# Block-sparse attention and a gated convolution FFN on one core: the diagonal matrices of the last convolution made on GpSimd instead of VectorE

## The chip, the core and the metric

One core of one Trainium2 chip. Its engines work side by side and meet at semaphores: TensorE (PE, matrix products into PSUM; PEld is its loading of weights), VectorE (DVE), ScalarE (ACT), GpSimd (POOL) and SyncE (SP), which here only issues transfers. Each engine takes its instructions strictly in the order in which the program gives them. The metric is device time of one execution in microseconds. A profile is one execution, recorded by the hardware; its span runs from the first to the last instruction.

## The reference

Inputs are q, k and v of 4 batches, 8 heads, 768 positions and 64 values per head, a table of 3 sampled key blocks for each of 24 query blocks, and the weights of a feed-forward part. Attention is computed under a mask of 32x32 blocks; what follows is a ReLU, a convolution of three taps along the positions, and a gate:

```python
scores = scale * np.matmul(q, k.transpose(0, 1, 3, 2))
mask = np.abs(blk_i - blk_j) <= window
mask = mask | (blk_i == 0) | (blk_j == 0) | (blk_i == n_blocks - 1) | (blk_j == n_blocks - 1)
for qb in range(n_blocks):
    for kb in sampled_blocks[qb]:
        mask[qb * block:(qb + 1) * block, kb * block:(kb + 1) * block] = True
scores = np.where(mask, scores, -1000000000.0)
...
out = np.matmul(attn, v)          # attn: softmax of scores
...
h = np.maximum(x @ w_in, 0.0)     # x: the heads side by side, 512 wide; h: 1024 wide
for k in range(K):                # K = 3
    conv_out += conv_w[k][None, None, :] * hp[:, k:k + S, :]
gate = 1.0 / (1.0 + np.exp(-conv_out))
return (h * gate @ w_out).astype(np.float32)
```

## The kernel before

The work is written as a graph of 1,811 small steps (`op`), each with a name, the engine or engines that may run it, and the buffers that it takes and uses. Nothing is scheduled when the kernel is built: the text `ORDER` lists all the steps in the order in which they are put down, two characters for the step, one for its engine where there is a choice, and one for each buffer that it takes (`put_down`, L94). A planner with its own table of costs has searched that order beforehand; the costs and due times that stand in the `op` calls are the planner's and do nothing at run time. So an engine's queue is the list of its steps in the order of the text.

Attention goes in units: for two heads at a time (a pair P, 16 pairs in all) and half of the positions, TensorE computes scores of 128x1024 into `st` (L773; the contraction of 88 rows is the 64 values of a head and 24 rows that carry the mask), ScalarE takes their exponential into `pt` (L785, 144 of them), and TensorE multiplies them with `vt` into `av` (L810). VectorE divides by the sum (L719, L721) into `xtok`. A segment is half a batch; the last half of the last batch is cut into one segment of 256 and one of 128 positions. For each segment `xtok` is transposed, multiplied with `winb` into `mix` (L914), put through the ReLU into `hE` (ScalarE L934 or VectorE L936), convolved and gated into `gT` (VectorE L972, L980, L1022, L1027, ScalarE L1019), multiplied with `woutb` (L844), copied to `o2s` and stored.

Keys and queries come in through GpSimd's transfer queue into `nat`. For the first pairs TensorE transposes them into `mix` or `av` and VectorE copies them into the slot `t` (L328 is the helper line for all plain copies of VectorE, L324 that of ScalarE, L326 that of GpSimd); later pairs are transposed by transfers into `stg` and copied from there. v comes into `vn` and is copied into `vt`. GpSimd's queue holds the issues of these loads (L239) in a fixed sequence; between them stand copies of one element, `pace` (L419, L685), that read a buffer and so keep a load from starting before that buffer has been written. In the first 15 us TensorE's queue also has 42 dummy products on `warm` (L230), of which the last 29 are named `fill`.

The convolution is done on VectorE, three multiplications with a tap each and two additions. In the last segment of 128 positions alone TensorE does it: for each of the 8 blocks of 128 channels and each of the 3 taps it multiplies `hE` with a diagonal matrix `diag` of 128x128, which carries the tap's weights of the channels (L991, 24 products). These 24 matrices are made by the steps `diag`, eight of them with three instructions each (L391): the identity `ident` times a column of `cw`. `cw`, the weights turned by one small transpose through `mix` (L381, L383), is ready at about 11 us, and the order puts the eight steps at 11.8, 13.1, 21.9 (two), 23.8, 26.9 (two) and 58.2 us.

Of the kernel before, what the change touches and what calls it, by code (L numbers as in the profile page):

```python
# [22 lines left out]
5l05m0z0T1ZV11+V5n21/020V21V5q15r5v01m11VV01n0W1t0ZV1u5s35w0A5e05f0B5E15F5x45G55j5k5o5J05K2a05L02bV22d12eV2fV2cV5O1
5P5p5t0C0D5Q15T05U0E1R15u0F0G0H5y6016127V15A014V5B1SV1TV5V25z16235H2n2k22y02g22A14V2B4W1w2u34X2M14Y2O04Z2P1x4+6505I
662o05M6742pV32qV6a16b6c55N5R2r16f06g5S5W5X2302sV2tV6k16l2lV2175Y15Z5C15DV024V630642zV325V1q6h06m16t06u68696d6e6y1
6z6i6j6v26A36n6o16D06E2h16F45+06w6I16J6x6B6C6G6R06S6H6K56L6M6W16X6T06Y11v1a2iV6p21r6q2jV6N05/V6O6r16/0706U06V6sV6P0
6QV71274175763in1io7907aiq0ir7i17j7b41p1sipV001d2NV4isViL07k51y4/2+2it17n07oiu6Z6+7p0iMiNiOivV1501z513025231531A54
1B5537056iP7s17t7273iw0ix7x07y2v17u1iyA393103211e330347z277787G17H7c2C02wV2xViT12DV47e12EViU7f7L07M7d17l7I37N4iQiF1
7Q17m7RiG7q7r7V07W7v7wiHV22F07AiR2GV2HV7S57X07B2Q17+17/7J0iz080187088892iA7K8c18d8e32RV0iWiViS0iBV32SV7C27O7P7T8h0
8i7U7Y7Z2T0iX2UV7D8m18j48n818302VViC18v0iDiEV8wiI0821iJiYiZ84iKVi/2j0j738o58x08A18B8a8b8f8g8F08G8C18H28k7g18l8p8q  # L30
8K17E08L8y08P08z7hA18M38518Q8D8E8I8R48r1j2i+7FVj18s86V8X18J8Y8Z58N8O8t0900912/V0j8j38Sja8uV8U235Vj9jl1951jm8T192096
8+8/939a09b94jf0jgj497136Vjbj538V1j69c2jc9i1989j9n0999o9d9ejhjn9k43c19p58Vjd9f0je9s19t9u1573a583b23d113g13hV2593i
3j12I03l3k5a3r3u3v02W13n08W2joji9x09yjjA0jpV19g3eV3fV1o9z39C1jr1jsju0jvjtAjwAjP09l09m9D2J19q9K09Ljx09E0jy9P19Q9M2
9R49r9v9wjQ2KV2LVjzVjSjR9A9U09V9B9FjA19H1jT9W59IjBjCAjX19Z19G19N9+jD0jG1jHa50jEjU9/1jZjVjYjFVj+a6jIAa739Oaa19Sabac0
jM12X09Taf0ag9XjN9Yak1alah4k322YVk42ZVk6j/am5jJ0ap0jKa0aqa1a80a9adax1aeaiajay3x3s23w3G3Dk0k5jLVa22jOVjWk1kb3a3k7k2
kckdkear2anaz1aoaC0aDaskp0aH1aIat1aAaE3aJ0k8aBaM0aFaNaGkB1aU1aKkCaLkqaVaO4aZ0aPaQa+kfkgaW5a/2k9kakrkDb219h9J3o3z13A
3m3a43y4au0khkiksb3kEktA2b433pV3BVkFV3avb70kK0b8kLb90kH13CV3qVbc1aX0kIbdaYkJV14kMAbe53H23E03J3I3S3P3Q13T33Vbk0blkQ0
b0kN1bm1b1kRb5kSAl30aR1l4aSl6l5l7kOkPA5lb1ld3tV3b6bp1bqbr4bakT0bu0bbl83L1jkkukG3M3W0aw03K0aT3UbvkW1kUkVV6bz1bw2bAbf
bg1kXbnbokYAbB3bsbH0kZ0bIbtbxk+bM1bybNl01bJ0k/A7lclj2lklml9bR0bCbSl1kj0bO5bh2lebil2V3FV43NVla1lflr3bW1bXbT1bY4kv1bD
kkb/0bK03RA0bE0llbFlslnc0c71c8c13kwbLbPbQbUkxbVbZb+c90lgcc0cdklkyce53XkzA0bGbjkAjqlulhltlvkmc2c31cach1cbciknV2lo3+  # L40
414213/24643lic41lplwlx3OVlqcj2lF1lz0cm0cnlGlAcu1cvcw1co4lBlHly3YV1lIlJV3cz1lClDV0cAcfcB3cE0lO1cFlPlL03ZVc540V1lQV
cG0lMlNAcgcJ1cKm70cO0cPckcllU1cpcqlVm8m9macr0cL5lR0lSmbcscQ2lWAlTAmf1mccx0cW1cycXcCc/0cDl+1l/d0cHcIcMcNcY4d41d5d13
d65mhmgmdmim0VcRcT2mjlX0lYcS1lZAcZd90c+m11dadh1d2dim40d3m2d7mkdb2dj3dm0dnm5d8dr1ds44454c4f4g04k4h4imemn2momlmqcUm3V
m6VmpkolKc61471lE4l048cVctdo1mJ1dcdw0dxdddk0dldt0dy4mv3mxmrmmmwde1mydfmzdB1dCdpmD0dqdJ0dKdumKdD5msdL3mEdO1dvdzdAdE
dF1dPmtmu4d04t4u2mAdT0dUdMmFdNmLdgdQ1dV0dRdY1mBmCmMdZmGe40dSe5mNV1dG2d+4dWdXm/1e91n04eV249V24aVn1V084j4y4q4r1e65
mHA2eaee0d/e0eb2n50efn21n34mmO4sV3dHe10e24z1dI2eg3ej1ekn6e70eo0epn4Vnn0n7V9np4nV3no4oVel1eq04v4H4I34w4x4E4M4J4F24K
4Lne1e8ew1ecexn80n9ey5edeheieB0nfeCemenereG1eHnaAeD2ngAnb0es1ezeL0nceMeAnh1nv1nqet1eI34S4T0eN1eunrndVanwnD2nxnEny
eT1eEeUnk0eFnieJeKeOePeY0nleV4eZnjAbnseQ2eRnGnz4pe3ev4AeS4N04Oe+0eW0f11nmAf2mP1eXmQe/mRf60f0f7mV0f35f4mSnAf82fb1mW
nFnL3nMnHnBntnOnNmTV3nP4GV44BV4nu0nCnIfcfd1fj0mXfkf5mYfl4fo1f9oc1fpft0odmZA0nQfq0oeVnJo90fafufeoao31obAfg0nK4CVo4
o5Afy1fzo60o7nZ1n+oz0nRfv3fA5o8AoAnSfhoBor1otosoC4PV0ouoDov4QVfG0fHff1n/o0fI2fL1fMoi0fmfnfQ0fRo1A1ojfrof1ogfsfN1fw  # L50
fxfV1fWfS4okAohAoEoH2owfX0nT0ol1fBfCfJ0f+0f/g03fKomfOfPnUg61fTg7g85nVoIoxonVoJoyoFoKgb0gcoo1opfUfD1oLfYfZgg1ghg1nW
oqVfE4UV0gd2o2fi0m+4b4DfFmU4RoMgi1oP3oQg32oGoRoSg4oTgl0gmg21gn4p11g9gt1gugagep2gfgjgy0gkgzgogv0nXA1gA3oUgpgw0gxoX0
gD1gEgM0gBoYgF5gq0groNoOoVoWgNgCp3oZgR1gSgO2gGgHgP1o+gT1o/A0p4gW0gXgY4h31h4gI1gJp5V3gK0pd1pepfpgh80gLV1gsg5nYh9gQ
h50phA1p0mIp6ha3pj0pm1pkpnplA1cpoApH1pIpJpKhd1hehf5hm0pp0ps1pqptgUhnhr1gVprAdpuAgZpy0g+h60h7ho2pLpMpP0g/0pQpRpNpSh0
hbhspv1hw0pzhcht1hxpwhghhpAApxAepThi2pX2pYhjp+pO1pZhy4hF1pB0pChGp71p8pDAfp9hK0h10pahp1hLhqhuhvhH0pUpVp/h2ApbA0hzhA
hk0hB1hlVpE1pFhM3hChT1hD0hUi00hI0hJpGApWhEVq33q0q4q5q6q1qq1hNhP0hO1i1qw0qrhV5i22qsAgq7q8hWq2i51i6hXhY2ie0ifqH1q9qb1
qxqcqdqaig1qyAhhZqIqX0hQqKqYqeqn0qoi31i4i74i8qfA2qpAii90hR1ihiihSA2ia1ibqz2qAqBqCij0qDikqt0ic1quidAqh1qvAjqih+0qj
h/Ail0qkqEimAqlA3rl0rmrnAqP3qQqFqJqGqLq+qSqRrr1rsrtAqMrx1ru0rvryro1rprH0rwArz2qNqTrAqOqZrBrIr30rqArC1rDr4r91raqgpc
piqmqUrE1rJ2q/qVr0rFqWrGr1rKrM1sd0s71rNrbr5s8serO3r2rLrPrcrQrdA2s9r6r7V0rR1rSsfrTrUsasgrf0rgrVA1sbA3shArer8rWscsirh
rirjArkrX1rYrZr+s11r/Vs0s2s3s4s5As6  # L60
"""


# [49 lines left out]
def kernel(  # L113
# [149 lines left out]
    o_ident = op("ident", {"POOL": 0.31}, lambda e: nc.gpsimd.affine_select(  # L263
        out=ident, in_=ident, compare_op=ALU.not_equal, fill=1.0, base=0,
        pattern=[[-1, 128]], channel_multiplier=1), -19, [o_imem], after=[o_iota])
# [120 lines left out]

    o_diag = {}
    for f in sorted({f for prs in CONV_PE.values() for pr in prs for f in (2 * pr, 2 * pr + 1)}):
        def dg(e, f=f):
            for x in range(3):  # L390
                nc.vector.tensor_scalar(out=diag[:, x, f], in0=ident, scalar1=cw[:, x, f:f + 1], scalar2=None,  # L391
                                        op0=ALU.mult)
# [683 lines left out]
```

## Time and profile before

| | |
|---|---|
| median of 3 runs | 207.18 us (206.76 to 207.27) |
| the profiled execution | 207.02 us |
| its span | 205.2 us |
| granted TensorE clock, mean | 0.998 |
| busy, TensorE | 200.1 us, 98% of the span |
| busy, ScalarE | 189.4 us, 92% |
| busy, VectorE | 184.7 us, 90% |
| busy, GpSimd | 60.0 us, 29%; nothing after 133.9 us |
| the 24 instructions L391 on VectorE | 4.6 us together |
| TensorE's first use of a diagonal matrix | 192.7 us |

Busy time is the union of the instructions' spans on an engine. A row of the timeline gives start, length, engine, line, operation, what is written and read, and how often; in brackets the idle time ahead of it and what ended that. A group's row gives busy time, the mean length of one in ns, and idle time ahead. A row of the chain gives start, length and what the end of the program waited for there. A busy TensorE is not one at its peak, since the ends of its instructions are modelled.

### The profile page before, as it was taken

The numbers are of one execution on the slowest core, as the hardware profiler recorded it, in microseconds if no ns is written. First come the engines' busy times: TensorE is split into PE (matmuls) and PEld (weight loads), VectorE is DVE, ScalarE is ACT, GpSimd is POOL, SyncE is SP. The second block draws the span as 40 slices with busy tenths as digits, with TensorE's granted clock in tenths as the row PEclk, the third lists the DMA queues.
The fourth block names the chain that finished last, engine by engine and source line by source line (L and its number), as shares of the span: only waits on it lengthen the run. The fifth ranks groups of instructions, "written<-read, shape, count | busy, mean of one in ns | idle before, by whom it ended". The sixth has DMA issues, their size and how long they took to land.

```text
span 205.2 us, 6315 instructions
## 1 busy us (share of the span) xinstructions
PE 200.1 (98%) x2442; PEld 145.2 (71%) x2442; DVE 184.7 (90%) x577; ACT 189.4 (92%) x252; POOL 60.0 (29%) x116
## 2 busy tenths in 40 slices
PE   7999999999999999999999999999999999999994
PEld 5678877877677766766477667766676767787773
DVE  6999999999999998999899979999999737999970
ACT  5899999999999999999799999999999989998843
POOL 5987634326242423114215334710000000000000
PEclk9999999999999999999999999999999999999999
DMA  6999997999989995999969779994040260001305
GB/s 148 191 179 193 188 201 119 143 120 148 144 110 113 124 143 73 244 123 127 222 106 171 116 103 180 133 136 77 0 139 21 78 227 0 3 0 71 139 29 179
DMA packets 50913, 25.45 MB, mean 124 GB/s; under 512 B 35588, under 2 KB 48740, under 8 KB 50884
## 3 DMA queue, kind: packets, MB, share of 16 engines
q0 software_dynamic: 20000, 11.24, 44.5%
q1 hardware_dynamic: 30452, 13.45, 32.8%
q8 instruction: 19, 0.31, 0.6%
q10 hardware_dynamic: 432, 0.36, 0.6%
q14 instruction: 10, 0.08, 0.1%
HBM read 23.09 MB, written 6.29 MB: 143 GB/s over the span
## 4 chain that ended last, share of the span: by engine, by line
PE 78%; ACT 14%; DVE 4%; issue 3%; ACTq 0%
PE st L773 25%; PE mix L914 18%; PE mix L844 15%; PE av L810 13%; ACT pt L785 10%; PE av L230 2%; DVE t L328 2%; ACT hE L934 2%; ACT m L1019 1%; PE st L844 1%; PE mix L740 1%; PE av L991 1%; ACT o2s L324 1%; DVE diag L391 1%; PE mix L536 1%
## 5 line engine op out<-in xcount | busy, mean ns | idle before, releaser
L785 ACT ACTIVATE pt<-st 128x1024 bf16<-128x1024 f32 x144 | 140.3, 1033 | 4.5 <-PE st L773 3.3
L773 PE MATMUL st<-t 88*128 88x256 bf16 (+2 forms) x600 | 93.0, 268 | 0.5 <-ACT pt L785 0.3
L810 PEld LDWEIGHTS <-pt 128*128 128x128 bf16 x1152 | 55.4, 97 | 13.7 <-ACT pt L785 0.4
L773 PEld LDWEIGHTS <-t 88*128 88x128 bf16 x600 | 48.6, 97 | 20.6 <-issue 1.0
L810 PE MATMUL av<-vt,pt 128*128 128x65 bf16 x1152 | 62.4, 193 | 0.1
L914 PE MATMUL mix<-xT,winb 128*128 128x384 bf16 (+2 forms) x288 | 55.7, 308 | 0.1
L972 DVE TENSOR_SCALAR m<-hE,cw 128x382 bf16<-128x382 bf16 (+2 forms) x192 | 49.9, 318 | 3.8 <-ACT hE L934 3.6
L844 PE MATMUL mix<-woutb,gT 128*128 128x512 bf16 (+2 forms) x200 | 49.6, 360 | 0.0
L980 DVE TENSOR_TENSOR m<-m 128x764 bf16<-128x764 bf16 (+2 forms) x64 | 33.4, 531 | 0.2
L914 PEld LDWEIGHTS <-winb 128*128 128x128 bf16 x288 | 24.1, 97 | 8.6 <-issue 0.7
L1019 ACT ACTIVATE m<-m 128x764 bf16<-128x764 bf16 (+2 forms) x32 | 26.2, 826 | 0.0
L844 PEld LDWEIGHTS <-gT 128*128 128x128 bf16 x224 | 18.7, 97 | 8.8 <-DVE gT L1027 0.3
L419 POOL COPY pace<-pt 1x1 bf16<-1x1 bf16 x24 | 7.6, 317 | 50.3 <-ACT pt L785 50.1
L934 ACT ACTIVATE hE<-mix 128x384 bf16<-128x384 f32 (+2 forms) x39 | 18.9, 504 | 0.9 <-PE mix L914 0.4
L721 DVE TENSOR_TENSOR xtok<-av,rcp 128x384 bf16<-128x384 f32 (+2 forms) x36 | 18.2, 507 | 0.3
L1027 DVE TENSOR_TENSOR gT<-m,hE 128x764 bf16<-128x764 bf16 (+3 forms) x36 | 18.0, 508 | 0.3
L239 POOL DMA_DIRECT2D nat<-in_q_dram x23 | 16.9, 736 | 2.0 <-issue 1.6
L936 DVE TENSOR_SCALAR hE<-mix 128x384 bf16<-128x384 f32 x25 | 13.8, 554 | 1.0 <-PE mix L914 0.7
L328 DVE COPY t<-mix 64x384 bf16<-64x384 bf16 (+1 forms) x34 | 13.8, 410 | 0.8 <-PE mix L536 0.2
L1022 DVE TENSOR_SCALAR m<-m 128x764 bf16<-128x764 bf16 (+3 forms) x36 | 12.1, 342 | 0.6 <-ACT m L1019 0.5
L239 POOL DMA_DIRECT2D vn<-in_v_dram x16 | 11.5, 720 | 1.3 <-issue 0.6
L328 DVE COPY t<-stg 64x1536 bf16<-64x1536 bf16 x20 | 11.6, 586 | 0.3
(74 smaller groups left out, 118.9 us busy)
## 6 DMA issues: line engine op xcount, KB each, us to landing
out_dram<-o2s SPq DMA_DIRECT2D x16, 256.0 KB
vn<-in_v_dram POOLq DMA_DIRECT2D x16, 192.0 KB, 5.1
nat<-in_k_dram POOLq DMA_DIRECT2D x15, 192.0 KB, 5.0
out_dram<-o2s SPq DMA_DIRECT2D x15, 128.0 KB
nat<-in_q_dram POOLq DMA_DIRECT2D x6, 192.0 KB, 4.9
winb<-in_moe_w_in_dram POOLq DMA_DIRECT2D x2, 512.0 KB, 7.6
woutb<-in_moe_w_out_dram POOLq DMA_DIRECT2D x4, 256.0 KB, 7.3
nat<-in_q_dram POOLq DMA_DIRECT2D x9, 96.0 KB, 4.9
```

Of the source, the lines that this page charges most:

```text
L239: return op(name, {eng: occ}, lambda e: on(e).dma_start(out=dst(), in_=src), prio, deps, dma=(kind, service), **kw)
L328: nc.vector.tensor_copy(out=dst, in_=src)
L721: nm = op("norm", {"DVE": t_dps(128 * C)}, lambda e: nc.vector.tensor_tensor(out=xtok_t[xk.index][:, 0:C].rearrange("p c h d -> p h c d"), ...
L773: nc.tensor.matmul(out=st[:, 128 * x:128 * (x + n_)], lhsT=t[0:88, 12 + 6 * hh + kc, :], rhs=t[0:88, idx:idx + (n_ - 1) * (2 if P < NPE el ...
L785: nc.scalar.activation(out=pt_t[ptb.index][:, c0:c1], in_=st_t[stb.index][:, c0:c1], func=AF.Exp, bias=0.0, scale=0.125)
L810: nc.tensor.matmul(out=o[:, off:off + 65], lhsT=pt_t[ptb.index][:, 128 * x:128 * x + 128], rhs=V_t[vslot_b[P].index][:, hh, kc, 0:65], sta ...
L844: nc.tensor.matmul(out=acc(), lhsT=gT_t[gb.index][:, ffc, 128 * t:128 * t + 128], rhs=woutb[:, ffc, c0:c1], start=(ffc == 0), stop=(ffc == ...
L914: nc.tensor.matmul(out=mix_t[hb.index][:, w1 * y:w1 * y + w1], lhsT=winb[:, fc, 128 * ffc:128 * ffc + 128], rhs=xT_t[xt_buf[n].index][:, f ...
L934: nc.scalar.activation(out=dst, in_=src, func=AF.Relu, bias=0.0, scale=0.5)
L972: nc.vector.tensor_scalar(out=m_t[cb.index][:, x, y, 0:w], in0=hE_t[heb.index][:, f0 + y, t0 + x:t0 + x + w], scalar1=cw[:, x, f0 + y:f0 + ...
L980: nc.vector.tensor_tensor(out=m[:, a_, :, 0:w], in0=m[:, a_, :, 0:w], in1=m[:, b_, :, 0:w], op=ALU.add)
L1019: th = [op("tanh", {"ACT": t_act(2 * w) + 0.04}, lambda e, cb=cb, w=w: nc.scalar.activation(out=m_t[cb.index][:, 0, :, 0:w], in_=m_t[cb.in ...
```

## The change

The step `diag` goes from VectorE to GpSimd, and its place in the order from the first third to the end of GpSimd's queue, behind the last load of v. The order of the first third was searched again with that.

```diff
-                nc.vector.tensor_scalar(out=diag[:, x, f], in0=ident, scalar1=cw[:, x, f:f + 1], scalar2=None,
+                nc.gpsimd.tensor_scalar(out=diag[:, x, f], in0=ident, scalar1=cw[:, x, f:f + 1], scalar2=None,
                                         op0=ALU.mult)
-        o_diag[f] = op("diag", {"DVE": 3 * t_d4(128)}, dg, T(10 + f), [o_cw, o_ident], earliest=14.0)
+        o_diag[f] = op("diag", {"POOL": 1.2}, dg, T(100 + f), [o_cw, o_ident], earliest=130.0)
```

The text `ORDER` differs in its first fifth (to about 65 us), and behind that only in the numbers of buffers, which are handed out in another rotation, and in the eight places where the GpSimd steps now stand. Decoded by engine, the orders differ so:

- VectorE: the 24 instructions are gone. In the early part a copy of mask rows (`m_r1`, one L328 of 24x384) stands ahead of the key copies of the third pair, which followed the second `diag` step before; `ident24` and `cw` come a few steps later, and other steps change places with near neighbours.
- TensorE: the last eight `fill` products come earlier by up to 30 steps, several products `av` stand later among the score products, and transposes and products into `mix` change places with near neighbours.
- ScalarE: four steps change places with near neighbours (two `tanh`, one copy into `xT`, one ReLU).
- GpSimd: one load of v (the fifth) stands two loads later, one load of q ahead of a load of `winb` and a `pace`; a few `pace` copies change places; the eight `diag` steps stand last.
- SyncE: one transfer of mask rows stands two places earlier, one transposing transfer one place earlier.

More of the change, by code (lines that the diff above doesn't have):

```diff
@@ L22 @@
 0V0h0i0j1G01HA00YA0XA0k0l0m1M11NV1IV12V191c0n0o1J01KA1LV0p0q0r0s0t5b00u5c0v5g10w5h1Q02m32211l161O01PV5d05i11Y10x0y
[L23 to L60, printed above, removed]
+5l05m0z0A0B1/05q10C1ZV11+V2n5n220V21V1VV00T0D5r0E0F5v05w5s30G5e01m15E15F5f0H5j5x40W0ZV14V1n5G55J05K2a05k2d15O15P5o
@@ new lines @@
+5L02bV22eV2fV2cV27V15Q15p5t5u5T05U5y1R1601615V25z16232k22g22A12y04V2B4W2u31w4X2M14Y2O04Z2P1x4+5A01SV171TV5B5H5I650
+665M2o06a16b2r15N6742pV32qV6c52sV2tV5R5S6f06g6h05W5C06k16l5X2lV25Y163064686t06u6m1692315Z24V5DV02zV325V6y16z6d6v26e
+6i6A36j6D06E5+06n6o12h16F46I16J6w6x6B6C6R06S6G6H6K56L6M6W16X6T06Y16p25/V6q2iV2jV6N06O6r06U06/06P1706V6sV6QV1d1a712
+74175in0763io7907aiq1ir7i17j7b4ipV007k51y4/2+26Z6+7n07oit0iu7p0501z513025231531A541B55370562NV4isViL0iMiNivV1iOiP
+7s17tiw1ix72737x07y7u1iyA3931e10321330343c17z27G12v07H7778iT12wV2xV7I3iQ7c2C17d17L07l7M7e12DV42EViF07m7qiG7Q17r7R7v
@@ new lines @@
+7N47w2F17A7V07W7fiUiHV27S52GV2HV2Q07B7+17/iz17J07X087088iA7K8018c18d892iW2RV0iV2SV8e3iBV37C2iX7O2T07P7T7DiRiY7U2UV
+iC17Y7Z8h02VV8i8j48m1iD818n830iEV848218a8o58b7E08v08w7g18f8g8A18k8l8p8B8x07hA18C18F08q8y08GiI1iJ8K18L8H28M3iS0iZi/2
+j12/V08r2j07FViKVj28508z8P08Qjf18R48s86V8X18Y8t08D8E8I900918J8N8O8Z5j73j8j38uV35Vi+jaj99209518S8T1jl08+969a09b8/93
+j497194jmjg36Vjbj5j638V19c2jc989i1999j9n09d9e9ojhjn9k49p59s19t9u1573a583d3b23g13i593j13l2I03k3ujd8U1je9f0113hV2joji
+9x09yjjA0jpV19g3eV3fV8V9z3ju0jvjwAjr1js9l19C19m9DjtAjP09K09E09L9qjx0jy9r9P19Q9M29R5jQjRjSjzV9v2J19w9A9U09V2KV2LV9B
@@ new lines @@
+9FjA09H2jT9W19IjBjCAjX1jU9Z1jD19+9G09/3jZjG0a50jH9NjVjY3n08W23v05a2W13rjEjFVj+a6jIAa749Oaa19Sabac0jM02X19Taf0ag9XjN
+9Yak1alah5k322YVk42ZVk6j/am1jJ1ap0jKa0aqa1a81a9adax1aeaiajay3x3s23w3G3Dk0k5jLVa21jOVjWk1kb3a3k7k2kckdkear2anaz3ao
+aC0aDaskp1aH1aIat0aAaE4aJ0k8aBaM0aFaNaGkB0aU1aKkCaLkqaVaO5aZ0aPaQa+kfkgaW1a/2k9kakrkDb219h9J3o3z13A3m3a43y4au0khki
+ksb3kEktA2b443pV3BVkFV3avb70kK1b8kLb90kH03CV3qVbc1aX1kIbdaYkJV14kMAbe13H23E03J3I3S3P3Q13T33Vbk0blkQ1b0kN0bm3b1kRb5
+kSAl30aR2l4aSl6l5l7kOkPA5lb1ld3tV3b6bp1bqbr5bakT1bu0bbl83L1jkkukG3M3W0aw03K0aT3UbvkW0kUkVV6bz1bw2bAbfbg0kXbnbokYA
@@ new lines @@
+bB4bsbH0kZ1bIbtbxk+bM1bybNl00bJ0k/A7lclj2lklml9bR0bCbSl1kj1bO1bh1lebil2V3FV43NVla1lflr3bW1bXbT3bY5kv0bDkkb/0bK13RA0
+bE0llbFlslnc0c71c8c14kwbLbPbQbUkxbVbZb+c90lgcc0cdklkyce13XkzA0bGbjkAjqlulhltlvkmc2c30cach1cbciknV2lo3+414213/24643
+lic42lplwlx3OVlqcj2lF0lz1cm0cnlGlAcu1cvcw3co5lBlHly3YV1lIlJV3cz1lClDV0cAcfcB4cE0lO0cFlPlL13ZVc540V1lQVcG0lMlNAcgcJ1
+cKm70cO0cPckcllU0cpcqlVm8m9macr0cL1lR1lSmbcscQ2lWAlTAmf1mccx1cW1cycXcCc/0cDl+0l/d0cHcIcMcNcY5d41d5d14d61mhmgmdmim0V
+cRcT1mjlX1lYcS0lZAcZd90c+m10dadh1d2dim41d3m2d7mkdb2dj4dm0dnm5d8dr1ds44454c4f4g04k4h4imemn2momlmqcUm3Vm6VmpkolKc61
@@ new lines @@
+471lE4l048cVctdo3mJ0dcdw0dxdddk1dldt0dy5mv3mxmrmmmwde2mydfmzdB1dCdpmD1dqdJ0dKdumKdD1msdL4mEdO1dvdzdAdEdF0dPmtmu4d0
+4t4u2mAdT0dUdMmFdNmLdgdQ3dV0dRdY1mBmCmMdZmGe40dSe5mNV1dG1d+5dWdXm/0e91n04eV249V24aVn1V084j4y4q4r1e61mHA2eaee0d/e0
+eb2n51efn20n34mmO4sV3dHe10e24z1dI2eg4ej1ekn6e71eo0epn4Vnn0n7V9np4nV3no4oVel3eq04v4H4I34w4x4E4M4J4F24K4Lne0e8ew1ecex
+n81n9ey1edeheieB0nfeCemenereG1eHnaAeD2ngAnb1es0ezeL0nceMeAnh0nv1nqet2eI44S4T0eN3eunrndVanwnD2nxnEnyeT1eEeUnk1eFnieJ
+eKeOePeY0nleV5eZnjAbnseQ1eRnGnz4pe3ev4AeS4N04Oe+0eW1f11nmAf2mP0eXmQe/mRf60f0f7mV1f31f4mSnAf82fb1mWnFnL3nMnHnBntnOnN
@@ new lines @@
+mTV3nP4GV44BV4nu0nCnIfcfd3fj0mXfkf5mYfl5fo1f9oc0fpft0odmZA0nQfq0oeVnJ1to91fafufeoao30obAfg0nK4CVo4o5Afy1fzo61o7nZ0
+1un+oz0nRfv4fA1o8AoAnSfhoBor1otosoC4PV0ouoDov4QVfG0fHff0n/o0fI2fL1fMoi1fm1qfnfQ0fRo1A1ojfrof0ogfsfN3fwfxfV1fWfS5okA
+ohAoEoH2owfX0nT1ol01vfBfCfJ1f+0f/g04fKomfOfPnUg61fTg7g81nVoIoxonVoJoyoFoK1rgb0gcoo0opfUfD2oLfYfZgg1ghg1nWoqVfE4UV0
+gd2o2fi0m+4b4DfFmU4RoMgi3oP3oQg31oGoRoSg4oTgl0gm1pg20gn5p10g9gt1gugagep2gfgjgy0gkgzgogv0nXA1gA4oUgpgw11sgxoX1gD1gE
+gM0gBoYgF1gq0groNoOoVoWgNgCp3oZ1ogR1gSgO2gGgHgP0o+gT3o/A0p4gW0gXgY5h31h4gI2gJp5V3gK1pd0pepfpgh80gLV1gsg5nYh9gQh50
@@ new lines @@
+phA1p0mIp6ha4pj1pm0pkpnplA1cpoApH1pIpJpKhd1hehf1hm0pp1ps0pqptgUhnhr1gVprAdpuAgZpy1g+h61h7ho2pLpMpP0g/0pQpRpNpSh0hb
+hspv0hw0pzhcht3hxpwhghhpAApxAepThi1pX2pYhjp+pO1pZhy5hF1pB1pChGp70p8pDAfp9hK0h11pahp0hLhqhuhvhH0pUpVp/h2ApbA0hzhAhk1
+hB2hlVpE0pFhM4hChT1hD1hUi00hI1hJpGApWhEVq33q0q4q5q6q1qq0hNhP0hO0i1qw1qrhV1i22qsAgq7q8hWq2i51i6hXhY1ie0ifqH1q9qb0qx
+qcqdqaig3qyAhhZqIqX0hQqKqYqeqn1qoi30i4i75i8qfA2qpAii91hR0ihiihSA2ia2ibqz2qAqBqCij0qDikqt1ic0quidAqh0qvAjqih+1qjh/A
+il1qkqEimAqlA3rl1rmrnAqP3qQqFqJqGqLq+qSqRrr0rsrtAqMrx0ru1rvryro0rprH1rwArz2qNqTrAqOqZrBrIr31rqArC0rDr4r90raqgpcpiqm
@@ L61 @@
+qUrE1rJ2q/qVr0rFqWrGr1rKrM0sd0s71rNrbr5s8serO3r2rLrPrcrQrdA2s9r6r7V0rR0rSsfrTrUsasgrf1rgrVA1sbA3shArer8rWscsirhri
+rjArkrX0rYrZr+s11r/Vs0s2s3s4s5As6
 """
```

## The prediction

> **What bounds the kernel now.** I read the page first, then a table of stretches, then the chain of waits in the first 30 us, then the timelines of ScalarE, VectorE and GpSimd. The profiled execution took 207.02 us, of which its span is 205.2; the median of the runs shown is 207.18, so the profile stands 0.16 below it, and a change worked out on the span is added to 207.18. About 0.3% of it, 0.6 us, is what a measurement of this kernel can tell from no change.
>
> ```profile
> PE 200.1 (98%) x2442; PEld 145.2 (71%) x2442; DVE 184.7 (90%) x577; ACT 189.4 (92%) x252; POOL 60.0 (29%) x116
> PE 78%; ACT 14%; DVE 4%; issue 3%; ACTq 0%
> ...
> 15.00:25.00 10.00, 9.94 (x185) 8.60 (x184) 9.51 (x33) 9.61 (x11) 6.53 (x14) 1.00 1.34 191
> 25.00:35.00 10.00, 9.97 (x120) 7.36 (x118) 9.44 (x32) 9.80 (x12) 3.66 (x9) 1.00 1.07 167
> 134.00:144.00 10.00, 10.00 (x110) 6.53 (x109) 9.97 (x30) 10.00 (x15) 0.00 (x0) 1.00 0.73 102
> 144.00:154.00 10.00, 10.00 (x112) 6.72 (x111) 9.72 (x31) 9.94 (x16) 0.00 (x0) 1.00 0.23 71
> 154.00:164.00 10.00, 9.98 (x126) 7.10 (x125) 9.09 (x27) 9.69 (x12) 0.00 (x0) 1.00 0.19 50
> ```
>
> The columns of the table are the stretch, its length, then busy time and instructions of TensorE, its weight loads, VectorE, ScalarE and GpSimd. Three engines are full at once. TensorE carries 78% of the chain, VectorE 4%. So VectorE time that is freed is worth something only where VectorE is on the chain, and VectorE time that is added costs something wherever VectorE has no room. In 134 to 144 us it has none: 9.97 of 10, with GpSimd at zero. That is the stretch into which the change puts GpSimd's work.
>
> ```profile
> 11.12 0.62 DVE mtok L296
> 11.76 0.59 DVE diag L391 x3
> 12.37 0.72 DVE t L328
> 13.12 0.68 DVE diag L391 x3
> 13.80 0.62 DVE t L328 x2
> ...
> 14.85 0.33 PE mix L536 x3
> ...
> 16.12 0.76 ACT pt L785
> ...
> 20.77 0.81 ACT pt L785
> 21.67 0.84 ACT pt L785
> 22.58 0.83 ACT pt L785
> 23.48 1.07 ACT pt L785
> 24.59 0.42 PE av L810 x8
> ```
>
> This is the chain, in order of time. Up to 14.8 us it runs through VectorE, and two of the eight groups of diagonal matrices lie on it: 0.59 + 0.68 = 1.27 us. From 16.1 to 24.6 us it runs through ScalarE's exponentials, then through TensorE. The other six groups come later and are on no part of it.
>
> **What leaves VectorE.** Twenty-four instructions L391, which together keep it busy for 4.6 us.
>
> ```profile
> L391 DVE TENSOR_SCALAR diag<-ident,cw 128x128 bf16<-128x128 bf16 x24 | 4.6, 281 | 0.1
> 15.85 0.35 DVE L328 COPY t<-t 24x384 bf16<-24x384 bf16 x1
> 7.23 8.50 ACT L785 ACTIVATE pt<-st 128x1024 bf16<-128x1024 f32 x9 [0.28 <-PE st L773]
> 16.12 16.23 ACT L785 ACTIVATE pt<-st 128x1024 bf16<-128x1024 f32 x17 [0.39 <-PE st L773]
> 32.22 0.51 ACT L934 ACTIVATE hE<-mix 128x384 bf16<-128x384 f32 x1
> ```
>
> Of the 1.27 us on the chain the new order gives some back at once: decoding both orders, a copy of mask rows (the 0.35 us at 15.85) now stands ahead of the key copies that followed the diagonals. These copies therefore come 1.27 - 0.35 = 0.92 us earlier. What is late next is ScalarE. It takes an exponential every (23.48 - 20.77) / 3 = 0.903 us when it is fed. Its first nine fill 7.23 to 16.12, where 9 x 0.903 = 8.13 would do: 0.76 us can be won there, less than 0.92. Between 16.12 and 24.6 it is at its rate already (16.12 to 23.48 is 7.36 us, eight of them and 0.14 over). From 24.6 the chain is TensorE, full. So the likely gain of the first third is **0.7 us**. The other 3.3 us of freed VectorE time I cost at nothing; the cover is TensorE's own queue. Bounds: nothing, if the moved steps of TensorE (its attention products now stand later among the score products, eight dummy matmuls earlier) eat it; at most 0.76 plus what the 17 exponentials from 16.12 to 32.22 lose, 16.10 - 17 x 0.903 = 0.75, so 1.5 us.
>
> On GpSimd's queue one load of v and one load of q change places with neighbours in the first 20 us, a move by one or two issues of about 0.7 us; on SyncE's queue two issues move by one or two places. All of these loads are used well behind their landing, so I take nothing, up to 0.3 us either way.
>
> **What GpSimd gains.** The same 24 instructions, last in its queue.
>
> ```profile
> 133.17 0.72 POOL L239 DMA_DIRECT2D vn<-in_v_dram  x1 [0.28 <-DVE m L972]
> 1.25 0.29 POOL L263 TENSOR_SCALAR_AFFINE_SELECT ident<-ident 128x128 bf16<-128x128 bf16 x1 [0.28 <-DVE ident L224]
> 4.91 0.50 POOL L326 CAST nat<-o2s 128x384 bf16<-128x384 f32 x1 [1.14 <-DMA o2s<-in_k_dram]
> 6.09 0.35 POOL L326 CAST nat<-o2s 128x192 bf16<-128x192 f32 x1
> L991 PEld LDWEIGHTS <-diag x24: 95/97/98, 192.7 to 196.7; 128*128 128x128 bf16 x24
> ```
>
> The last load ends at 133.9. A GpSimd instruction of 128x128 took 0.29 us, one of 128x192 0.35, so 24 take 7.0 to 8.4 us and end near 142 us, or near 155 if they wait often. TensorE needs the first matrix at 192.7. Nothing stands behind them on GpSimd, so their own length costs nothing; the cover is about 40 us.
>
> **What they cost VectorE.** No row of before shows this instruction on GpSimd. The nearest rows are those in which the two engines met.
>
> ```profile
> 4.98 0.84 DVE L296 SCALAR_TENSOR_TENSOR mtok<-sbi,keyid,A 24x384 bf16<-24x384 int32 x1
> 11.12 0.61 DVE L296 SCALAR_TENSOR_TENSOR mtok<-sbi,keyid,A 24x384 bf16<-24x384 int32 x1
> 71.39 1.03 POOL L419 COPY pace<-pt 1x1 bf16<-1x1 bf16 x1 [1.20 <-ACT pt L785]
> 71.36 0.55 DVE L980 TENSOR_TENSOR m<-m 128x772 bf16<-128x772 bf16 x1
> 71.82 0.55 DVE L1027 TENSOR_TENSOR gT<-m,hE 128x772 bf16<-128x772 bf16 x1
> 72.30 0.88 DVE L972 TENSOR_SCALAR m<-hE,cw 128x386 bf16<-128x386 bf16 x2
> ```
>
> GpSimd's copy of a single element, issued under two VectorE instructions that read SBUF twice, took 1.03 us and ended when the second of them had (72.37). The other way round, a VectorE instruction that began at 4.98 under GpSimd's cast of 4.91 to 5.41 took 0.84 us where its twin took 0.61. So each engine holds the other up. The price for VectorE: 0.23 us behind a cast of 384 elements, which means that it went on at 5.21, 0.20 before the cast's end. From the two casts (0.50 and 0.35 us) an element costs 0.15 / 192 = 0.78 ns and the rest, 0.20 us, does not depend on the size; so VectorE waited for the element part alone, 0.30 us. For 128 elements that part is **0.10 us**.
>
> How often? In 134 to 144 us VectorE starts 30 instructions; 25 of them read SBUF alone and are of the kinds that met above (L972, L980, L1022, L1027 and the copies from stg and vn).
>
> ```profile
> L980 DVE TENSOR_TENSOR m<-m 128x764 bf16<-128x764 bf16 x6 | 3.2, 548 | 0.0
> L972 DVE TENSOR_SCALAR m<-hE,cw 128x382 bf16<-128x382 bf16 x11 | 2.8, 314 | 0.0
> DVE hE L936 <- PE mix L914: 0.2, 1, 0.2
> 158.23 0.53 DVE L1027 TENSOR_TENSOR gT<-m,hE 128x772 bf16<-128x772 bf16 x1
> 159.13 0.38 PE L844 MATMUL mix<-woutb,gT 128*128 128x512 bf16 x1
> ```
>
> Since VectorE always has the next one ready (0.0 idle in these groups), nearly every GpSimd instruction is let in ahead of one: 24 x 25/30 = 20 times 0.10 us, **2.0 us** by which VectorE falls behind. Bounds: nothing, if the 0.10 us always fits into the gaps between VectorE's instructions; 24 x 0.23 = 5.5 us, if each costs as much as the cast did. I take 2.0 because it is scaled from the one pair of twins that differ by GpSimd's presence.
>
> VectorE's room to absorb it: its only wait between 134 and 158 us is 0.2 us for TensorE, and the gate product that ends at 158.76 is read by the output projection at 159.13, 0.37 us later. Together up to 0.5; I take 0.4. What is behind it goes to TensorE, which is full there. So **2.0 - 0.4 = 1.6 us** lost at about 159 us, and it is not regained: in 154 to 164 us VectorE has some idle time (9.09 of 10), but TensorE has none (9.98).
>
> The sum: -0.7 + 1.6 = **+0.9 us**, 207.18 + 0.9 = **208.1 us**.
>
> One rule speaks against this kind of move. The Trainium skill, "Perfetto Trace Analysis", section "Optimizing Scalar/DVE Operations", says that since GpSimd's only SBUF port is VectorE's second one, offloading between the two might not help. The rows at 4.98 and 71.39 agree that they block each other; by that rule alone the sum would be no gain, about 207.2.
>
> **Rivals.** *The gaps take it in.* GpSimd's 24 instructions slip between VectorE's, or under the few that read PSUM, and cost less than the 0.4 us of room; then only the gain is left: 207.18 - 0.7 = 206.5, at best 207.18 - 1.5 = 205.7. For it: the two VectorE instructions at 71.36 and 71.82 took 0.55 us each, though GpSimd stood waiting under them. Against it: the pair right behind, at 72.30, took 0.88 us, where one of its kind takes 0.31 on average (a load was issued there too), and a one-element copy has almost nothing to move. It decides if VectorE falls behind by less than 0.4 us in all. Chance 0.31.
>
> *The two cancel.* A delay of about 1 us (half of the meetings), less 0.4, against a gain of 0.6: 207.2. Chance 0.15.
>
> *The whole instruction blocks.* If GpSimd keeps VectorE out for its whole 0.29 us and not only for the element part, 20 x 0.29 = 5.8, less 0.4, less 0.7, is +4.7: 211.9. The cast's twins speak against it (0.23 lost of the 0.43 that were left of the cast). The Trainium skill, "SBUF — State Buffer", section "Who interferes with whom", states this rule: whoever issues first has the shared port pair for its whole instruction, and the other blocks fully. Chance 0.09.
>
> **How the numbers follow.** The forecast (+0.3 to +3 us) has 0.45. Faster by over 0.3% is the first rival, 0.31; within 0.3% the second, 0.15; slower by over 0.3% the forecast and the third, 0.54. The likeliest case's own range, with delays of 1.4 to 3.5 and gains of 0.3 to 1.0, is 207.5 to 210.0. For 8 in 10 the range takes in most of the first rival: 206.2 to 210.2.
>
> **What would show it.** Right: L391 on GpSimd from about 134 us, spans well over 0.3 us; L972, L1022 and the stg copies in 134 to 146 longer than before, by some 2 us together; a new wait of TensorE for gT or for a mix bank at 140 to 164 us; the ninth exponential followed by the tenth 0.7 us earlier. Wrong: VectorE's groups as long as before in that stretch; or TensorE's chain in the first 30 us no shorter, or shorter by over 1 us.

## The result and the profile after

The changed kernel takes 208.51 us (median of 6 runs, 208.02 to 208.62) against 207.23 us for the kernel before beside it: a ratio of 1.0064, with a 95% interval of 1.0048 to 1.0081. It is slower by 1.3 us. Its profiled execution took 208.27 us, with a span of 206.5.

First the early part. The rows are ScalarE's timeline after, then the same place before (start, length, engine, line, count).

```profile
7.34 24.65 ACT L785 ACTIVATE pt<-st 128x1024 bf16<-128x1024 f32 x26 [0.35 <-PE st L773]
31.86 0.51 ACT L934 ACTIVATE hE<-mix 128x384 bf16<-128x384 f32 x1
32.24 1.05 ACT L785 ACTIVATE pt<-st 128x1024 bf16<-128x1024 f32 x1
```

```profile
32.60 3.10 ACT L785 ACTIVATE pt<-st 128x1024 bf16<-128x1024 f32 x3
```

The wait between the ninth and the tenth exponential is gone; 26 run as one group. From the first to the 27th it is 32.24 - 7.34 = 24.90 us, before 32.60 - 7.23 = 25.37: 0.47 us won. The first itself came 0.11 later, so 0.36 is left on the clock, and in this profile it stays: the last load of v is issued at 132.82, before at 133.17.

Then GpSimd's timeline and VectorE's groups between 133.6 and 154.8 us, first after, then before.

```profile
132.82 0.72 POOL L239 DMA_DIRECT2D vn<-in_v_dram  x1 [0.28 <-DVE m L972]
133.58 21.21 POOL L391 TENSOR_SCALAR diag<-ident,cw 128x128 bf16<-128x128 bf16 x24
...
L972 DVE TENSOR_SCALAR m<-hE,cw 128x386 bf16<-128x386 bf16 (+1 forms) x27 | 8.4, 371 | 0.1
L980 DVE TENSOR_TENSOR m<-m 128x764 bf16<-128x764 bf16 (+1 forms) x10 | 5.3, 553 | 0.0
L328 DVE COPY t<-stg 64x1536 bf16<-64x1536 bf16 x4 | 2.3, 586 | 0.1
L1027 DVE TENSOR_TENSOR gT<-m,hE 128x764 bf16<-128x764 bf16 x4 | 2.1, 554 | 0.0
L1022 DVE TENSOR_SCALAR m<-m 128x764 bf16<-128x764 bf16 (+1 forms) x5 | 2.1, 429 | 0.0
...
L328 DVE COPY vt<-vn 128x768 bf16<-128x768 bf16 x1 | 0.4, 440 | 0.0
```

```profile
L972 DVE TENSOR_SCALAR m<-hE,cw 128x386 bf16<-128x386 bf16 (+1 forms) x30 | 7.8, 322 | 0.1
L980 DVE TENSOR_TENSOR m<-m 128x764 bf16<-128x764 bf16 (+1 forms) x10 | 5.2, 547 | 0.0
...
L328 DVE COPY t<-stg 64x1536 bf16<-64x1536 bf16 x4 | 2.2, 549 | 0.1
L1022 DVE TENSOR_SCALAR m<-m 128x764 bf16<-128x764 bf16 (+1 forms) x6 | 2.0, 354 | 0.0
...
L328 DVE COPY vt<-vn 128x768 bf16<-128x768 bf16 x1 | 0.4, 354 | 0.0
```

The 24 multiplications take 21.2 us on GpSimd, 0.884 each. In the same stretch VectorE's multiplications and its plain copies from SBUF are longer by 7 to 24%: L972 by 49 ns, L1022 by 75, the copies by 37 and 86. On the 30, 6, 4 and 1 that the kernel before does there, this makes 1.47 + 0.45 + 0.15 + 0.09 = 2.2 us. The additions L980 are hardly longer (6 ns). So VectorE falls behind, and others wait for it. Here are VectorE's gate product that stood at 158.23 before, a stretch of the table, and the waits of all engines between 134 and 164 us, after the change.

```profile
159.88 0.52 DVE L1027 TENSOR_TENSOR gT<-m,hE 128x772 bf16<-128x772 bf16 x1
...
144.00:154.00 10.00, 9.39 (x96) 6.06 (x97) 9.87 (x28) 8.58 (x14) 10.00 (x12) 1.00 0.23 70
...
PEld L773 <- issue: 1.0, 2, 0.7
ACT m L1019 <- DVE m L980: 0.8, 1, 0.8
PEld L914 <- issue: 0.6, 1, 0.6
ACT hE L934 <- PE mix L914: 0.6, 1, 0.6
PE st L773 <- DVE t L328: 0.5, 1, 0.5
PEld L844 <- DVE gT L1027: 0.5, 1, 0.5
PE mix L914 <- DVE hE L936: 0.4, 1, 0.4
```

The gate product comes 1.65 us later though the last load was 0.35 earlier: VectorE is 2.0 us behind (the wait of 0.2 us for TensorE that it had there before has gone, which makes up the rest of the 2.2). ScalarE, busy for 9.94 of 10 us in 144 to 154 before, is busy for 8.58. TensorE and its weight loads wait for VectorE at three places (a ReLU, a gate product, a copy from `stg`) and ScalarE at one, where before none of these waits was there. On the chain VectorE's share goes from 4% to 12%:

```profile
PE 59%; ACT 20%; DVE 12%; issue 5%; DMA 1%; SPq 1%; ACTq 0%
```

VectorE's last instruction tells what is left of this at the end (after, then before):

```profile
203.18 0.29 DVE L328 COPY o2s<-mix 128x128 f32<-128x128 f32 x1 [2.23 <-PE mix L844]
201.84 0.29 DVE L328 COPY o2s<-mix 128x128 f32<-128x128 f32 x1 [2.23 <-PE mix L844]
```

From the last load of v to it, it is 203.18 - 132.82 = 70.36 us, before 201.84 - 133.17 = 68.67: **1.69 us** lost behind the load. Less the 0.35 by which the load came earlier, this is the 1.3 us.

### The profile page after: what moved, and what is told of

Read it like the earlier page. It is cut to its first block, busy times and chain, and to the rows that moved or that the text cites. A ratio compares the mean times of both kernels' runs of the same rounds, so it can differ in the third digit from the quotient of the medians.

```text
span 206.5 us, 6295 instructions
## 1 busy us (share of the span) xinstructions
PE 199.6 (97%) x2423; PEld 145.4 (70%) x2442; DVE 182.9 (89%) x553; ACT 189.5 (92%) x252; POOL 80.6 (39%) x140
## 4 chain that ended last, share of the span: by engine, by line
PE 59%; ACT 20%; DVE 12%; issue 5%; DMA 1%; SPq 1%; ACTq 0%
PE st L773 19%; ACT pt L785 15%; PE mix L914 12%; PE mix L844 11%; PE av L810 11%; DVE m L972 4%; PE av L230 2%; DVE m L980 2%; ACT m L1019 2%; ACT hE L934 2%; DVE t L328 1%; DVE gT L1027 1%; DMA stg<-nat 1%; PE st L844 1%; DVE hE L936 1%
## 5 line engine op out<-in xcount | busy, mean ns | idle before, releaser
L972 DVE TENSOR_SCALAR m<-hE,cw 128x382 bf16<-128x382 bf16 (+2 forms) x192 | 51.5, 326 | 3.9 <-ACT hE L934 3.6
L844 PE MATMUL mix<-woutb,gT 128*128 128x512 bf16 (+2 forms) x181 | 46.4, 358 | 0.8 <-DVE gT L1027 0.2
L980 DVE TENSOR_TENSOR m<-m 128x764 bf16<-128x764 bf16 (+2 forms) x64 | 33.5, 532 | 0.2
L391 POOL TENSOR_SCALAR diag<-ident,cw 128x128 bf16<-128x128 bf16 x24 | 21.2, 896 | 0.0
L328 DVE COPY t<-mix 64x384 bf16<-64x384 bf16 (+1 forms) x34 | 13.8, 410 | 1.1 <-PE mix L536 0.3
L1022 DVE TENSOR_SCALAR m<-m 128x764 bf16<-128x764 bf16 (+3 forms) x36 | 12.2, 346 | 0.6 <-ACT m L1019 0.5
```

The lines of the kernel that those rows point to most:

```text
L391: nc.gpsimd.tensor_scalar(out=diag[:, x, f], in0=ident, scalar1=cw[:, x, f:f + 1], scalar2=None, op0=ALU.mult)
L844: nc.tensor.matmul(out=acc(), lhsT=gT_t[gb.index][:, ffc, 128 * t:128 * t + 128], rhs=woutb[:, ffc, c0:c1], start=(ffc == 0), stop=(ffc == ...
L972: nc.vector.tensor_scalar(out=m_t[cb.index][:, x, y, 0:w], in0=hE_t[heb.index][:, f0 + y, t0 + x:t0 + x + w], scalar1=cw[:, x, f0 + y:f0 + ...
L980: nc.vector.tensor_tensor(out=m[:, a_, :, 0:w], in0=m[:, a_, :, 0:w], in1=m[:, b_, :, 0:w], op=ALU.add)
```

## The experiments

Each kernel was timed beside the kernel before in five rounds; a ratio is to that, with its 95% interval. The kernel before had medians of 206.94, 207.06 and 206.93 us in the three sets of rounds (the first four experiments, the next four, the last three); a ratio can differ from the quotient of two medians by some 0.2%. Profiles of one and the same program start with some scatter (the last experiment shows it), so places in a profile are compared inside it.

**The order alone.** One group of diagonal matrices instead of eight.

```diff
-            for x in range(3):
+            for x in range(3 if f == 5 else 0):
...
-lhsT=diag[:, x, f0 + y]
+lhsT=diag[:, x, 5]
```

> The changed kernel with only one of the eight groups of diagonal matrices made (three instructions instead of 24); the last convolution uses that one group for all eight channel blocks, so its products take the same time and the output of the last 128 positions is another. Theory P (VectorE and GpSimd hold each other up in 133 to 155 us, nothing else costs): the 1.65 us lost there shrinks to about 3/24 of it, within VectorE's room, so only the early gain of 0.35 us is left: 206.9 us (206.6 to 207.1), L972 in 134 to 155 us as long as before. Theory O (the order searched anew and its other rotation of buffers cost the time further down, the meeting of the engines does not): 208.2 to 208.6, as the changed kernel.

Measured: 207.15 us, 0.9992 (0.9971 to 1.0013). The loss of 1.3 us is gone although order and rotation of buffers are those of the changed kernel, so these do not cause it; theory O falls here. The gain of 0.35 us is too small to be told from nothing at this interval.

**The same order, the matrices on VectorE where it waits.** Two groups at 163 us, six at 166, by their places in `ORDER`.

```diff
-nc.gpsimd.tensor_scalar(out=diag[:, x, f], ...
+nc.vector.tensor_scalar(out=diag[:, x, f], ...
```

> The changed kernel's order, but all 24 instructions on VectorE again, put where VectorE waits: two groups behind the last gate product of the third batch (about 163 us), six behind the copy into xT at about 168 us, where VectorE waited 3.4 us for ScalarE. Theory P: 24 x 0.163 us of VectorE time go into idle time, GpSimd has nothing behind 133 us: 206.9 us (206.6 to 207.2). Theory O: 208.2 or more. A third case: the six groups run 0.2 us past the hole and hold up the last segments: 207.2 to 207.5.

Measured: 207.20 us, 0.9999 (0.9979 to 1.0018); the profiled execution took 206.79, with a span of 204.7. The loss is gone, as P has it. The time is at the upper end of P's range, and the gain that the profile shows is not told from nothing.

**The matrices on GpSimd later.** All 24 multiplications, held back by a copy that reads the third batch's last gate product.

```diff
+            if f == 5:
+                nc.gpsimd.tensor_copy(out=pace_t, in_=gT_t[gt_buf[2].index][0:1, 7, 700:701])
             for x in range(3):
```

> The changed kernel, but GpSimd's 24 instructions wait behind a one-element copy that reads the last gate product of the third batch, so that they start at about 164 us, where VectorE has 4.4 us idle in 6. Theory P: they are shorter there than the median 0.72 us of the changed kernel (0.3 to 0.6), VectorE's L972 in 134 to 155 us are as long as before, and the time is 206.9 (206.6 to 207.3, the end of the 24 meeting VectorE again behind 170 us). Theory O: 208.2 or more. If GpSimd slows something other than VectorE by its mere running: 207.8 or more.

Measured: 208.26 us, 1.0052 (1.0033 to 1.0071). The time misses P's range and would fit O, which the two runs above had ruled out; the profile says why. GpSimd first, then VectorE, and then VectorE's same instructions in the kernel before:

```profile
163.54 14.78 POOL L393 TENSOR_SCALAR diag<-ident,cw 128x128 bf16<-128x128 bf16 x24
...
L393 POOL TENSOR_SCALAR diag<-ident,cw x24: 592/594/835, 163.5 to 177.5; 128x128 bf16<-128x128 bf16 x24
...
170.20 3.11 DVE L974 TENSOR_SCALAR m<-hE,cw 128x382 bf16<-128x382 bf16 x6 [3.43 <-ACT hE L936]
173.23 1.19 DVE L982 TENSOR_TENSOR m<-m 128x764 bf16<-128x764 bf16 x2
```

```profile
170.34 1.62 DVE L972 TENSOR_SCALAR m<-hE,cw 128x382 bf16<-128x382 bf16 x6 [3.43 <-ACT hE L934]
171.88 1.14 DVE L980 TENSOR_TENSOR m<-m 128x764 bf16<-128x764 bf16 x2
```

Undisturbed, one multiplication takes 0.594 us (the row's middle number), twice what the prediction had taken. So about 11 of 24 fit between 163.5 and 170.2, and the rest meet VectorE again: a run of six multiplications takes 3.11 us instead of 1.62. These 1.5 us are about all that this kernel loses (the table at the end of the experiments has 1.45). P's condition, that the end meets VectorE again, had come true at a higher price than it allowed.

**The old order, the matrices on GpSimd.** Only the eight steps move.

```diff
-nc.vector.tensor_scalar(out=diag[:, x, f], ...
+nc.gpsimd.tensor_scalar(out=diag[:, x, f], ...      # and the eight steps behind the last load in ORDER
```

> The kernel before, its order untouched but for the eight groups, which go to the end of GpSimd's queue. Theory P: VectorE falls behind by 2.0 us in 133 to 155 us as in the changed kernel, TensorE loses 1.65 us of it, and the early gain without a new order is 0 to 0.7 us (two groups of 1.27 us were on the chain): 208.2 to 208.9. Theory O: as before, 207.2 or less, since the order is the old one.

Measured: 208.66 us, 1.0073 (1.0049 to 1.0097). The loss needs no new order. And the early gain needs none:

```profile
7.51 24.65 ACT L784 ACTIVATE pt<-st 128x1024 bf16<-128x1024 f32 x26 [0.36 <-PE st L772]
32.42 1.05 ACT L784 ACTIVATE pt<-st 128x1024 bf16<-128x1024 f32 x1
```

From the first to the 27th exponential it is 24.91 us, 24.90 with the order searched anew.

**Half as many.** Four groups at the changed kernel's place, and the same four in VectorE's quiet stretch.

```diff
-            for x in range(3):
+            for x in range(3 if f in (2, 5, 6, 7) else 0):
...
-lhsT=diag[:, x, f0 + y]
+lhsT=diag[:, x, (5, 6, 2, 7)[(f0 + y) // 2]]
```

> The changed kernel with four of the eight groups made (12 instructions on GpSimd from 133 us); the last convolution uses each of them for two channel blocks, so its output there is another. Theory D (the loss grows with the number of meetings): VectorE falls behind by 12 x 0.083 = 1.0 us, of which its room takes 0.35, so 206.9 + 0.65 = 207.5 us (207.3 to 207.7). Rival L (only the later meetings, near the tight places at 144 to 153 us, cost): the 12 end at about 144 us and VectorE catches up, 206.9 to 207.1.

> The same 12 instructions and the same conv on four groups, but started at 163.5 us behind a one-element copy that reads the last gate product of the third batch, so that they fall into the 6.7 us in which VectorE does little. Theory P (it is the meeting that costs, not GpSimd's running): 12 x 0.6 = 7.2 us, so one or two of them meet VectorE behind 170 us: 206.9 to 207.2, and VectorE behind by 0.3 us at most. Rival: the last segments are short of time anyhow and any work on GpSimd there costs: 207.5 or more.

Measured: 206.93 us, 0.9989 (0.9966 to 1.0012), at the early place; 206.64 us, 0.9973 (0.9951 to 0.9994), at the late one. The first time lies in L's range, and not in D's (207.5); its profile speaks for D all the same (the table at the end of the experiments). The late 12 cost nothing, and that kernel, which makes half of the matrices, is faster than the one before.

```profile
163.19 6.98 POOL L393 TENSOR_SCALAR diag<-ident,cw 128x128 bf16<-128x128 bf16 x12
```

Three, 12 and 24 multiplications from 133 us give 0.9992, 0.9989 and 1.0064: by the times alone, a loss is seen only with 24. The early half differs from the late half by 0.29 us in the medians, which the intervals do not separate.

**Writing only.** 24 fills instead of multiplications.

```diff
-nc.gpsimd.tensor_scalar(out=diag[:, x, f], in0=ident, scalar1=cw[:, x, f:f + 1], ...
+nc.gpsimd.memset(diag[:, x, f], 0.0)
```

> The changed kernel with GpSimd's 24 multiplications replaced by 24 fills of the same 128x128 matrices with zero, at the same place: it writes the same bytes and reads nothing of SBUF; the last convolution then multiplies with zeros, so the output there is another. Theory W (what blocks VectorE's fast instructions is the shared way in either direction): L972 in 133 to 150 us longer than its 0.316 us still, a loss in proportion to the fills' length; if they take 0.3 us each, 207.3 to 207.8. Rival R (GpSimd's reads are what blocks): L972 as long as ever, 206.9.

Measured: 206.80 us, 0.9972 (0.9939 to 1.0005).

```profile
133.86 4.58 POOL L391 MEMSET diag<- 128x128 bf16 x24
...
L971 DVE TENSOR_SCALAR m<-hE,cw 128x382 bf16<-128x382 bf16 x10 | 2.8, 348 | 0.0
```

and VectorE's same ten in the kernel before:

```profile
L972 DVE TENSOR_SCALAR m<-hE,cw 128x382 bf16<-128x382 bf16 x10 | 2.6, 331 | 0.0
```

A fill takes 0.19 us (the median; the longest of those that meet a multiplication takes 0.31), and VectorE's multiplications under the fills (133.9 to 138.5 us) take 0.348 on average, 17 ns over the 0.331 of the same stretch before: lengthened as W has it, but for ten instructions only, 0.2 us, which VectorE's room takes in. So instructions that only write hold VectorE up too, if little; the time fits R. What makes a multiplication dearer, its two reads or its greater length, this run leaves open.

**One read and no scalar.** The same matrices by a select.

```diff
-nc.gpsimd.tensor_scalar(out=diag[:, x, f], in0=ident, scalar1=cw[:, x, f:f + 1], ...
+nc.gpsimd.affine_select(out=diag[:, x, f], in_=cw[:, x, f:f + 1].broadcast_to([128, 128]),
+                        compare_op=ALU.is_equal, fill=0.0, base=0, pattern=[[-1, 128]], channel_multiplier=1)
```

> The changed kernel with each matrix made by one select instead of a multiplication: GpSimd reads the column of weights, stretched over 128 columns, and keeps it on the diagonal, zero elsewhere. The same values, one input and no pointer to a scalar; the select that makes ident took 0.29 us against 0.594 for the multiplication where nothing disturbed it. Theory T (the loss goes with the time that GpSimd holds the shared way): VectorE behind by 1.0 us instead of 2.0, 207.3 to 207.7. Rival N (each meeting costs the same, however short): 208.2 to 208.6.

Measured: 207.50 us, 0.9997 (0.9969 to 1.0026). The time is in T's range (the kernel before had 207.06 in these rounds). The profiled execution took 208.20 us, the longest of the twelve. The rows are GpSimd's selects, and VectorE's additions and multiplications between 134.7 and 142.4 us.

```profile
134.46 7.91 POOL L391 TENSOR_SCALAR_AFFINE_SELECT diag<-cw 128x128 bf16<-128x128 f32 x24
...
L981 DVE TENSOR_TENSOR m<-m 128x764 bf16<-128x764 bf16 x6 | 3.7, 625 | 0.0
L973 DVE TENSOR_SCALAR m<-hE,cw 128x382 bf16<-128x382 bf16 x11 | 3.1, 342 | 0.0
```

Here the additions get longer too, 0.625 us where they take 0.548 in that stretch of the kernel before; the multiplications take 0.342 instead of 0.317.

**The select in the quiet stretch.** Both edits together, the start held back to 163 us.

> All 24 matrices made by the select on GpSimd, started at about 163.5 us behind a one-element copy that reads the last gate product of the third batch; the order of the first third as in the changed kernel. Theory P (only the meeting costs): 24 x 0.3 us = 7.2 us, nearly all of it in the 6.7 us in which VectorE does little, the early gain of 0.45 us is kept: 206.7 us (206.4 to 207.0). Rival: selects behind 170 us meet the run of L972 there and cost as much as the late multiplications did: 207.5 or more.

Measured: 206.68 us, 0.9980 (0.9965 to 0.9995). It makes all the matrices and is faster than both kernels, than the one before by 0.2%.

```profile
163.04 5.91 POOL L393 TENSOR_SCALAR_AFFINE_SELECT diag<-cw 128x128 bf16<-128x128 f32 x24
...
7.11 24.60 ACT L788 ACTIVATE pt<-st 128x1024 bf16<-128x1024 f32 x26 [0.25 <-PE st L776]
31.96 1.05 ACT L788 ACTIVATE pt<-st 128x1024 bf16<-128x1024 f32 x1
```

Undisturbed the 24 take 5.9 us and are done at 169, ahead of the run at 170; 31.96 - 7.11 = 24.85 us is the early gain again.

**The old order, VectorE late, and the kernel before once more.** Nothing on GpSimd; then no edit at all.

> The kernel before with its own order and nothing on GpSimd; only the eight groups on VectorE move, two behind the last gate product of the third batch and six behind the copy into xT at about 168 us, where it waits. Theory F (the early gain comes from VectorE being rid of the two groups on the chain, and the order searched anew adds nothing): the tenth exponential 0.4 to 0.5 us earlier against the first than in the kernel before, and 206.7 us (206.4 to 207.0), as with the new order. Rival S (the search brought the gain): 207.0 to 207.3.

> The kernel before, unchanged, profiled and timed once more beside these two: it shows by how much the first exponential (7.06 to 7.72 us in the profiles so far) and the time between the first and the tenth move from one execution to the next with the same program. If the early gain is real, its tenth exponential starts 8.8 to 8.95 us behind the first again (8.89 in the first profile, 8.34 to 8.51 in the kernels without the early groups). If the start alone scatters, its span is 204.9 to 205.6 us. Rival: the distance scatters as well, and the gain is not told from it.

Measured: 206.87 us, 0.9996 (0.9976 to 1.0016), and 207.11 us, 1.0005 (0.9982 to 1.0029). First the old order with late matrices, then the kernel before:

```profile
7.20 24.71 ACT L784 ACTIVATE pt<-st 128x1024 bf16<-128x1024 f32 x26 [0.25 <-PE st L772]
32.16 1.05 ACT L784 ACTIVATE pt<-st 128x1024 bf16<-128x1024 f32 x1
```

```profile
7.04 8.50 ACT L785 ACTIVATE pt<-st 128x1024 bf16<-128x1024 f32 x9 [0.25 <-PE st L773]
15.92 16.28 ACT L785 ACTIVATE pt<-st 128x1024 bf16<-128x1024 f32 x17 [0.38 <-PE st L773]
32.45 1.05 ACT L785 ACTIVATE pt<-st 128x1024 bf16<-128x1024 f32 x1
```

The unchanged kernel has its tenth exponential 8.88 us behind the first, as in its first profile (8.89), and the 27th 25.41 behind it (25.37). With the groups gone it is 24.96 in the old order, and 24.80 to 25.04 in all eleven profiles without the early groups. So the early gain is 0.3 to 0.6 us there, with either order: F stands, S falls. As a time it is at the edge of what these rounds tell: with the matrices late on VectorE it does not show (0.9996, 0.9999), with the late selects and the late half it does.

**All profiles from one mark.** The issue of the last load of v, just ahead of GpSimd's early matrices, parts each profile in two (us, from the starts in the timelines; the gate product is the one that stood at 158.23, the last copy is VectorE's last instruction).

| kernel | first exponential to last load | last load to gate product | last load to last copy |
|---|---|---|---|
| before, twice | 125.94, 126.00 | 25.06, 25.06 | 68.67, 68.66 |
| 24 on GpSimd at 133 us, new and old order | 125.48, 125.48 | 27.06, 27.07 | 70.36, 70.37 |
| 12 there | 125.44 | 25.77 | 69.26 |
| 3 there | 125.64 | 25.06 | 68.67 |
| 24 selects there | 126.01 | 25.87 | 69.45 |
| 24 fills there | 125.84 | 25.07 | 68.67 |
| 24 on GpSimd at 163 us | 125.51 | 25.07 | 70.12 |
| 12 at 163 us; 24 selects there | 125.46, 125.45 | 25.07, 25.07 | 68.68, 68.67 |
| 24 late on VectorE, new and old order | 125.40, 125.55 | 25.07, 25.07 | 68.67, 68.67 |

Wherever GpSimd's work meets little or none of VectorE's, the last two columns agree within 0.02 us, so they tell losses that the times cannot. Half of the multiplications leave VectorE 0.71 us behind at the gate product of that profile, and 0.59 is lost at the end: D had forecast 0.65, and L's "VectorE catches up" falls. The early gain of about the same size hides it in the time. Selects put VectorE 0.8 us behind, 0.4 of the 2.0 of the multiplications, and undisturbed they take 5.91 us against 24 x 0.594 = 14.3, which is 0.4 too: as T has it. In the first column the early gain is there in nine of the eleven profiles; those of the fills and of the selects at 133 us lose most or all of it again ahead of the load, and why is open.

## Why the prediction was right

**The sum.** +0.9 us forecast, +1.3 measured, by the mechanism that was forecast: -0.35 at the last load and +1.69 behind it, where -0.7 and +1.6 had been put. So the miss lies in the early gain. Taking the matrices off GpSimd's place removes the loss, putting them there with the old order brings it back. The low end of the likeliest case's range was added up wrongly: 1.4 - 0.4 - 1.0 is 0, so 207.2, not 207.5.

**The early gain** was mis-sized: 0.7 us forecast, 0.47 in the profile. The step that failed is "what is late next is ScalarE": the 26 exponentials that now run as one group take 24.65 / 26 = 0.948 us each, not the 0.903 of a fed ScalarE. The chain after, in order of time, runs through TensorE alone from 10.25 to 24.6 us; these are its first and last pieces in that stretch:

```profile
10.25 0.68 PE st L773 x4
10.99 0.24 PE av L810 x4
...
24.23 0.42 PE av L810 x8
24.64 0.45 PE st L773 x4
```

So TensorE's queue set the end of what could be won, before ScalarE's rate did. That the search adds nothing was not foreseen in words, but the 3.3 us of VectorE time costed at nothing were worth nothing.

**GpSimd's own time** was forecast at 7 to 8.4 us, up to 20 with waits; it took 21.2, since one multiplication takes 0.594 us and not the 0.29 of a select of that shape, 14.3 for 24. The other 7 us are waits for VectorE's additions and gate products:

```profile
142.36 1.00 DVE L1027 TENSOR_TENSOR gT<-m,hE 128x764 bf16<-128x764 bf16 x2
L391 POOL TENSOR_SCALAR diag<-ident,cw 128x128 bf16<-128x128 bf16 x1 | 1.9, 1937 | 0.0
```

This multiplication, the longest of the 24, lies from 142.01 to 143.95 and ends 0.58 us, its own length, after the second gate product. Ten additions and four gate products of about 0.5 us stand in that stretch: 14 x 0.5 = 7.0, an estimate. It cost nothing by itself: the matrices were ready at 154.8, long before the last convolution.

**VectorE's delay** was forecast as 20 meetings of 0.10 us, 2.0 us, and came out at 2.0. The total was right, the way to it less so: the delay is spread over VectorE's own instructions, 37 to 86 ns on each copy or multiplication and almost nothing on the additions, which GpSimd waits out, and of which the estimate had counted every one as a meeting. That these two errors cancel was luck. The rival that GpSimd keeps VectorE out for its whole instruction (5.8 us even at 0.29 each) falls: 24 x 0.594 = 14.3 us of GpSimd's work cost VectorE 2.0. The Trainium skill, "SBUF — State Buffer", section "Who interferes with whom", has the one that comes second blocked fully, for VectorE's modes that use both of its ports; here GpSimd bore most of it (21.2 us instead of 14.3), and VectorE a seventh of GpSimd's undisturbed time. In the run of six at 170 us it went the other way: between 171 and 172 us GpSimd's multiplications took their own 0.593 us and VectorE's 0.655, twice their undisturbed 0.32.

**The room** of 0.4 us was about right (2.0 less the 1.69 that was lost), the place was not: the loss was put at 159 us, at the gate product, and it came between 143 and 155 us, at a ReLU that frees a `mix` bank, at another gate product and at a copy from `stg`.

**The rule** in the Trainium skill, "Perfetto Trace Analysis", section "Optimizing Scalar/DVE Operations", that offloading from VectorE to GpSimd might not help, holds for this place. The late selects show its limit: where VectorE waits anyhow, GpSimd's work was free (68.67 us behind the last load, as without it).

**Open** stays what decides how a meeting is shared. At 136.5 and 147.9 us runs of six and eight multiplications took 1.80 and 2.38 us instead of 1.47 and 1.93, less than a quarter more; the run at 170 us took nearly twice its time.

## What to carry to other kernels

Work that moves from VectorE to GpSimd is priced at the place where it lands: at VectorE's copies and multiplications between SBUF tensors there, and at what waits for them, and not by GpSimd's idle share. Look for a stretch in which VectorE waits for something else, and check that the whole batch fits into it, at the measured length of that very instruction. Freeing an engine gains only up to the next queue on the chain, which here was TensorE's.
